# Weight tiles of a fused attention and feed-forward kernel: casting DMAs from GpSimd's queue in place of sync-queue loads and GpSimd casts

## Chip, cores and metric

One core of a Trainium2 chip. The metric is the device time of one execution in microseconds. Profiles are one profiled execution each; their times count from the start of the span.

## The reference, cut

Attention over 8 batches x 8 heads (512 local tokens in a window of 32, 32 global tokens, head size 64), then a feed-forward layer on the 4352 x 512 result:

```python
s_ll = np.where(np.abs(pos[:, None] - pos[None, :]) <= 32, s_ll, -1e9)
a_l = softmax(concat([s_lg, s_ll]));  out_l = a_l @ concat([v_g, v_l])
...
h = x @ w_in                       # w_in 512 x 2048
g = h * np.clip(h + 3, 0, 6) / 6
return g @ w_out                   # w_out 2048 x 512
```

All inputs are fp32. The kernel computes in half precision, so both weight matrices (4 MB each) have to become fp16 in SBUF.

## The kernel before: the parts that matter

Heads are handled in pairs, four pairs to a batch (`NM = 4`). Each weight matrix is cut into 16 tiles of 128 x 512. A tile of w_in is numbered `i = 4*qd + m`: `m` is the block of the contraction, `qd` the quarter of the 2048 columns. One feed-forward unit `u1(c)` multiplies column block `c` of w_in and so needs the four tiles of quarter `c // 4`: blocks 0 to 3 need tiles 0 to 3, block 4 is the first to need tiles 4 to 7.

```python
def stage():                       # 16 staging buffers of 128 x 512 fp32
    return wrk.tile([P, 512], FP32, tag="stg", name="stg", bufs=NSTG)

def load_w(kind, i):               # sync queue, plain DMA into staging
    t = stage()
    nc.sync.dma_start(out=t, in_=moe_w_in[...])      # or moe_w_out[...]
    w_st[kind, i] = t

def cast_w(kind, i, eng):          # GpSimd: staging fp32 -> home fp16
    eng.tensor_copy(out=o, in_=w_st[kind, i])
...
# sync queue, in program order (cut): k, q, v of pairs 0 to 3, then
for i in range(4): load_w("in", i)
load_g(1, 4, "kg"); load(4, "kq")
for i in range(4, 8): load_w("in", i)
load(5, "kq"); load(4, "v")
for i in range(8, 12): load_w("in", i)
...
# GpSimd, in program order (cut); first() is the v cast and a shifted copy
cast(3, "kq", nc.gpsimd)
for p in range(1, NM): first(p, "v")
for i in range(4): cast_w("in", i, nc.gpsimd)
cast(4, "kq", nc.gpsimd); load_vg(1)
for i in range(4, 8): cast_w("in", i, nc.gpsimd)
...
# PE, in program order (cut)
emit_G(1, 4, "kg"); u1(3); kglob(1, nc.vector)
emit_T(4)                          # transposes of pair 4
u1(4)                              # first use of w_in tiles 4 to 7
emit_S4(4)                         # mask matmuls, then the scores of pair 4
emit_T(5); ...
```

The orders of all engines are pinned, so an engine runs its instructions in just this order.

The softmax here doesn't subtract the row's maximum and nothing guards it: scores larger than these inputs give would overflow.

## Time and profile before

| | before |
|---|---|
| median of the fast runs | 317.62 us (317.42 to 318.07; the first run, 523.46, is no fast run; with it the median is 317.85) |
| span in the profile | 315.8 us, mean granted clock 0.998 |
| PE / VectorE / ScalarE / GpSimd busy | 96% / 68% / 63% / 48% |
| PE's work in the first 50 us, counted in columns | about 35 us (the five tens of the prediction add up to 32.5: its count leaves the 64-row matmuls out) |

To read it: PE is the bound after about 50 us; before that PE, ScalarE and VectorE wait for each other. The weights come by this list of DMA issues (columns: what, queue, kind and count, KB of one, median us from issue to landing):

```profile
stg<-in_moe_w_in_dram SPq DMA_DIRECT2D x16, 256.0 KB, 6.0
stg<-in_moe_w_out_dram SPq DMA_DIRECT2D x16, 256.0 KB, 5.1
```

### The profile page before, as it was taken

Reading aid. Unit: us, or ns where it says so; the run is one execution under the profiler, and the core shown is the slowest. Engines: PE = TensorE matmul, PEld = TensorE weight load, DVE = VectorE, ACT = ScalarE, POOL = GpSimd, SP = SyncE. Lnnn points to the kernel's source line nnn. Section 1 sums busy time; section 2 is a strip of 40 time slices with the busy share of each in tenths; the row PEclk is TensorE's granted clock in tenths of the full one; section 3 lists DMA queues with packets and bytes.
Section 4 is the critical chain, followed back from the end, with each engine's and each line's share of the span. In section 5 each row is a group of like instructions: output and inputs, shape, how many; then the busy total and the mean of one; then the engine's idle time right before and its main releaser. Section 6 shows DMA issues by size and latency. Waiting matters only on the chain.

```text
span 315.8 us, 7343 instructions
## 1 busy us (share of the span) xinstructions
PE 304.3 (96%) x2688; PEld 161.9 (51%) x2688; DVE 213.9 (68%) x484; ACT 200.1 (63%) x417; POOL 152.6 (48%) x273
## 2 busy tenths in 40 slices
PE   6898899999999999999999999999999999999995
PEld 4554555545555555555555555555555544448444
DVE  5678688898765799569945996468943962479101
ACT  6657877887444985479844993589556941579000
POOL 3878987599866475764574558542511000000000
PEclk9999999999999999999999999999999999999999
DMA  7999999999999999999997999896642002100131
GB/s 207 243 295 333 302 300 317 213 185 211 217 201 238 180 183 191 180 229 193 181 154 152 215 187 205 177 232 106 114 103 86 17 19 83 66 2 1 37 98 66
DMA packets 140260, 53.05 MB, mean 168 GB/s; under 512 B 127552, under 2 KB 131904, under 8 KB 140224
## 3 DMA queue, kind: packets, MB, share of 16 engines
q1 hardware_dynamic: 138048, 52.32, 78.3%
q0 software_dynamic: 2176, 0.26, 2.0%
q8 instruction: 21, 0.34, 0.5%
q14 instruction: 15, 0.12, 0.2%
HBM read 35.13 MB, written 8.91 MB: 139 GB/s over the span
## 4 chain that ended last, share of the span: by engine, by line
PE 81%; DVE 8%; ACT 6%; issue 2%; DMA 2%; SPq 0%; POOL 0%
PE po L488 34%; PE psH L472 32%; PE psS L297 3%; DVE gt L479 3%; PE pav L383 2%; PE pav L386 2%; ACT t L477 2%; DVE xn L391 2%; DMA stg<-in_q_l_dram 2%; DVE E L304 2%; PE psSG L357 1%; PE psS L326 1%; ACT E L335 1%; PE po L500 1%; ACT E L301 1%
## 5 line engine op out<-in xcount | busy, mean ns | idle before, releaser
L488 PE MATMUL po<-wout,gt 128*128 128x512 f16 x528 | 122.6, 379 | 0.0
L472 PE MATMUL psH<-xt,win 128*128 128x512 f16 x512 | 119.6, 379 | 1.4 <-POOL win L174 1.0
L479 DVE SCALAR_TENSOR_TENSOR gt<-t,psH 128x512 f16<-128x512 f32 (+1 forms) x144 | 90.1, 652 | 20.9 <-ACT t L477 19.8
L477 ACT ACTIVATE t<-psH,half_col 128x512 f32<-128x512 f32 (+1 forms) x144 | 91.8, 670 | 18.0 <-PE psH L472 16.8
L472 PEld LDWEIGHTS <-win 128*128 128x128 f16 x576 | 53.1, 98 | 52.8 <-POOL win L174 1.8
L488 PEld LDWEIGHTS <-gt 128*128 128x128 f16 x528 | 48.4, 98 | 52.2
L304 DVE TENSOR_TENSOR E<-E,mk 128x512 f16<-128x512 f16 x96 | 51.3, 569 | 30.4 <-ACT E L301 29.0
L301 ACT ACTIVATE E<-psS 128x512 f16<-128x512 f32 x96 | 49.9, 605 | 13.5 <-PE psS L297 13.4
L492 ACT COPY ot<-po 128x512 f32<-128x512 f32 x16 | 9.4, 586 | 58.6 <-PE po L488 53.1
L140 POOL CAST kn<-stg 128x512 f16<-128x512 f32 x31 | 19.8, 640 | 34.7 <-DMA stg<-in_k_l_dram 33.1
L391 DVE TENSOR_TENSOR xn<-pav,rc 128x256 f16<-128x256 f32 x64 | 26.1, 422 | 1.3
L409 POOL TENSOR_TENSOR s<-Eg 128x128 f32<-128x128 f16 x24 | 10.4, 434 | 33.8 <-ACT Eg L358 32.6
L492 DVE COPY ot<-po 128x512 f32<-128x512 f32 x17 | 11.7, 690 | 21.2 <-PE po L488 21.1
L140 POOL CAST qn<-stg 128x512 f16<-128x512 f32 x31 | 20.3, 656 | 11.3 <-DMA stg<-in_q_l_dram 11.3
L140 POOL CAST vt<-stg 128x512 f16<-128x512 f32 x32 | 21.1, 658 | 9.7 <-DMA stg<-in_v_l_dram 9.4
L144 POOL COPY vb<-vt 64x512 f16<-64x512 f16 x32 | 20.2, 631 | 2.1
L383 PE MATMUL pav<-vt,E 128*128 128x65 f16 x256 | 20.1, 194 | 0.0
L386 PE MATMUL pav<-vb,E 128*128 128x65 f16 x256 | 19.9, 195 | 0.0
L335 ACT ACTIVATE E<-psS 128x512 f16<-128x512 f32 x32 | 16.9, 600 | 4.8 <-PE psS L326 4.8
L383 PEld LDWEIGHTS <-E 128*128 128x128 f16 x256 | 17.9, 99 | 3.4
L386 PEld LDWEIGHTS <-E 128*128 128x128 f16 x256 | 16.8, 97 | 3.2
L297 PEld LDWEIGHTS <-kT 64*128 64x128 f16 x384 | 10.9, 94 | 10.1 <-issue 8.1
(93 smaller groups left out, 274.1 us busy)
## 6 DMA issues: line engine op xcount, KB each, us to landing
stg<-in_k_l_dram SPq DMA_DIRECT2D x32, 256.0 KB, 3.5
stg<-in_q_l_dram SPq DMA_DIRECT2D x32, 256.0 KB, 4.1
stg<-in_v_l_dram SPq DMA_DIRECT2D x32, 256.0 KB, 4.9
out_dram<-ot SPq DMA_DIRECT2D x23, 256.0 KB, 3.6
stg<-in_moe_w_in_dram SPq DMA_DIRECT2D x16, 256.0 KB, 6.0
stg<-in_moe_w_out_dram SPq DMA_DIRECT2D x16, 256.0 KB, 5.1
out_dram<-ot SPq DMA_DIRECT2D x8, 192.0 KB, 3.9
out_dram<-ot SPq DMA_DIRECT2D x16, 64.0 KB, 2.4
```

The lines of the kernel that those rows point to most:

```text
L140: eng.tensor_copy(out=o, in_=s[c + "f"])
L297: nc.tensor.matmul(out=pss[2 * ch + e][:, w * P:(w + 1) * P], lhsT=kT[r, c0:c0 + P], rhs=qT[r, w * P:(w + 1) * P])
L301: nc.scalar.activation(out=E[:, ch, e], in_=pss[2 * ch + e], func=EXP, scale=qk_scale)
L304: nc.vector.tensor_tensor(out=E[:, ch, e], in0=E[:, ch, e], in1=mk[:, ch].rearrange("p w c -> p (w c)"), op=mult)
L383: nc.tensor.matmul(out=o, lhsT=E[:, 0, e, w * P:(w + 1) * P], rhs=vt[:, w, m, c], start=True, stop=False, skip_group_check=True)
L386: nc.tensor.matmul(out=o, lhsT=E[:, 1, e, w * P:(w + 1) * P], rhs=vb[:, (w - 1) % NT, m, c], start=False, stop=True, skip_group_check=True)
L391: nc.vector.tensor_tensor(out=xn[:, 2 * w2:2 * w2 + 2].rearrange("p w (e d) -> p w e d", e=2), in0=po[:, :, 1:1 + P].rearrange("p w (e d) ...
L472: nc.tensor.matmul(out=ps[:, 0:n], lhsT=w_in_t[m][:, c * P:(c + 1) * P], rhs=rhs(m), start=(m == 0), stop=(m == NM - 1), skip_group_check= ...
L477: nc.scalar.activation(out=t1[:, 0:n], in_=ps[:, 0:n], func=RELU, bias=half_col, scale=1.0 / 6.0)
L479: nc.vector.scalar_tensor_tensor(out=gts[c][:, 0:n], in0=t1[:, 0:n], scalar=1.0, in1=ps[:, 0:n], op0=amin, op1=mult)
L488: nc.tensor.matmul(out=po[t][:, 0:dm], lhsT=gts[c][:, t * P:(t + 1) * P], rhs=w_out_t[c // 4][:, c % 4], start=(c == 0), stop=(c == NC - 1))
L492: (nc.scalar.copy if t % 2 else nc.vector.tensor_copy)(out=ot, in_=po[t][:, 0:dm])
```

## The change

The intent: a DMA issued from GpSimd can cast, so the 32 staging loads and the 32 casts become 32 loads straight into the fp16 homes; the sync queue is left to k, q and v. The core of the diff (removals in the sync queue's list, and most of GpSimd's list, are cut):

```diff
-    def load_w(kind, i):
-        t = stage()
...
-    def cast_w(kind, i, eng):
...
+    def load_w(kind, *ts):
+        for i in ts:
+            if kind == "in":
+                qd, m = divmod(i, NM)
+                cs = slice(qd * 512, (qd + 1) * 512)
+                nc.gpsimd.dma_start(out=w_in_t[m][:, cs], in_=moe_w_in[m * P:(m + 1) * P, cs])
+            else:
+                nc.gpsimd.dma_start(out=w_out_t[i // 4][:, i % 4], in_=moe_w_out[i * P:(i + 1) * P, :])
...
     cast(3, "kq", nc.gpsimd)
-    for p in range(1, NM):
-        first(p, "v")
-    for i in range(4):
-        cast_w("in", i, nc.gpsimd)
+    load_w("in", 0, 1)
+    first(1, "v")
+    load_w("in", 2)
+    first(2, "v")
+    load_w("in", 3)
+    first(3, "v")
+    load_w("in", 4, 5)
     cast(4, "kq", nc.gpsimd)
     load_vg(1)
-    for i in range(4, 8):
-        cast_w("in", i, nc.gpsimd)
+    load_w("in", 6, 7)
     cast(5, "kq", nc.gpsimd)
+    load_w("in", 8, 9)
...
```

The orders of PE, VectorE and ScalarE stay as they were.

More of the change, by code (lines that the diff above doesn't have):

```diff
@@ L155, in load_vg @@
         nc.gpsimd.dma_start(out=vg[rg, b], in_=v_g[b].rearrange("h s d -> s h d"))
-    w_st = {}
-    def load_w(kind, i):
-        t = stage()
-        if kind == "in":
-            qd, m = divmod(i, NM)
-            nc.sync.dma_start(out=t, in_=moe_w_in[m * P:(m + 1) * P, qd * 512:(qd + 1) * 512])
-        else:
-            nc.sync.dma_start(out=t, in_=moe_w_out[i * P:(i + 1) * P, :])
-        w_st[kind, i] = t
-    def cast_w(kind, i, eng):
-        if kind == "in":
-            qd, m = divmod(i, NM)
-            o = w_in_t[m][:, qd * 512:(qd + 1) * 512]
-        else:
-            o = w_out_t[i // 4][:, i % 4]
-        (eng.copy if eng is nc.scalar else eng.tensor_copy)(out=o, in_=w_st[kind, i])
+    def load_w(kind, *ts):
[6 more added lines that the diff above has]
+                nc.gpsimd.dma_start(out=w_out_t[i // 4][:, i % 4], in_=moe_w_out[i * P:(i + 1) * P, :])
     gst = {}
@@ L539 @@
         load(p, "v")
-    for i in range(4):
-        load_w("in", i)
     load_g(1, 4, "kg")
     load(4, "kq")
-    for i in range(4, 8):
-        load_w("in", i)
     load(5, "kq")
     load(4, "v")
-    for i in range(8, 12):
-        load_w("in", i)
     load(6, "kq")
@@ L552 @@
     load(7, "kq")
-    for i in range(12, NC):
-        load_w("in", i)
     load(6, "v")
@@ L557 @@
     load_g(0, 4, "qg")
-    for i in range(8):
-        load_w("out", i)
     load(2 * NM, "kq")
-    for i in range(8, NC):
-        load_w("out", i)
     load(2 * NM, "v")
@@ L621 @@
     cast(3, "kq", nc.gpsimd)
-    for p in range(1, NM):
-        first(p, "v")
-    for i in range(4):
-        cast_w("in", i, nc.gpsimd)
+    load_w("in", 0, 1)
[5 more added lines that the diff above has]
+    load_w("in", 4, 5)
     cast(4, "kq", nc.gpsimd)
     load_vg(1)
-    for i in range(4, 8):
-        cast_w("in", i, nc.gpsimd)
+    load_w("in", 6, 7)
     cast(5, "kq", nc.gpsimd)
+    load_w("in", 8, 9)
     first(4, "v")
     ones_v(1, nc.gpsimd)
-    for i in range(8, 12):
-        cast_w("in", i, nc.gpsimd)
+    load_w("in", 10, 11)
     cast(6, "kq", nc.gpsimd)
+    load_w("in", 12, 13)
     first(5, "v")
+    load_w("in", 14, 15)
     cast(7, "kq", nc.gpsimd)
-    for i in range(12, NC):
-        cast_w("in", i, nc.gpsimd)
+    load_w("out", 0, 1)
     first(6, "v")
+    load_w("out", 2, 3)
     first(7, "v")
+    load_w("out", 4, 5)
     vgsum(0, nc.gpsimd)
@@ L644 @@
     vgsum(1, nc.gpsimd)
+    load_w("out", 6, 7)
     load_vg(2)
-    for i in range(8):
-        cast_w("out", i, nc.gpsimd)
+    load_w("out", 8, 9, 10, 11)
     cast(2 * NM, "kq", nc.gpsimd)
-    for i in range(8, NC):
-        cast_w("out", i, nc.gpsimd)
+    load_w("out", 12, 13, 14, 15)
     units += moe_units(lambda mm: xts[0][mm], Sl, local_dests(0), early=True)
```

## The prediction

> **What bounds the kernel now.** I began with the page of the profile: busy shares first, then the 40 slices, to see whether one limit holds over the whole span.
>
> ```profile
> PE 304.3 (96%) x2688; PEld 161.9 (51%) x2688; DVE 213.9 (68%) x484; ACT 200.1 (63%) x417; POOL 152.6 (48%) x273
> ...
> PE   6898899999999999999999999999999999999995
> ...
> POOL 3878987599866475764574558542511000000000
> ...
> DMA  7999999999999999999997999896642002100131
> ```
>
> PE is busy 96%, yet those ends are modelled, so I also counted work: columns streamed over 2.4 columns per ns (the rate that eight 512-column matmuls in 1.73 us show), half for 64-row ones that run in pairs. This gives 3.8 of the first 10 us, 5.3 of the second, then 7.5, 7.3, 8.6 and 10.2. So PE has about 17 us of slack before 50 us and almost none after. Whatever this change does must happen before about 50 us: from there the matmuls stand back to back, and a shift at 50 us reaches the end unchanged. The DMA engines are full from about 4 us to 100 us.
>
> Next, the source view of the cast that the change removes (L174, GpSimd), and who waited for it:
>
> ```profile
> L174 POOL CAST win<-stg x16: 609/614/807, 17.8 to 38.9; 128x512 f16<-128x512 f32 x16
> L174 POOL CAST wout<-stg x16: 611/616/619, 45.0 to 57.6; 128x512 f16<-128x512 f32 x16
> ...
>   PEld L472: 1.8, 2
>   PE psH L472: 1.0, 2
> ```
>
> The 32 casts cost GpSimd 0.61 us each, 19.7 us in all. PE waited for them 1.0 us in total. The timeline of PE shows where: the third and fourth matmul of column block 4, which need the w_in tiles 6 and 7.
>
> ```profile
> 26.08 0.39 PE L472 MATMUL psH<-xt,win 128*128 128x512 f16 x1 [0.45 <-POOL win L174]
> 27.03 0.39 PE L472 MATMUL psH<-xt,win 128*128 128x512 f16 x1 [0.56 <-POOL win L174]
> 27.26 1.03 PE L310 MATMUL psS<-mneg,ident 128*128 128x512 f16 x4
> 28.48 0.62 PE L326 MATMUL psS<-qT,kT 64*128 64x128 f16 x16 [0.20 <-DVE kT L252]
> ```
>
> Last, the chain of work that ended last, in order of time, over the same stretch. It passes through VectorE and not through the cast: the scores at 28.48 wait for kT, behind the three gt and four kgT copies. Even the 1.0 us of PE is therefore not wholly on the path.
>
> ```profile
> 24.05 1.88 DVE gt L479 x3
> ...
> 26.93 0.69 DVE gt L479
> ...
> 27.83 0.61 DVE kT L252
> 28.44 0.05 issue
> 28.48 0.44 PE psS L326 x8
> ```
>
> **What the Trainium skill says.** (1) "DMA: Bandwidth & Descriptors", section "SWDGE vs HWDGE vs iDMA": a cast inside a DMA can only be issued from GpSimd, whose cores write the descriptors. That is why these loads leave the sync queue. The kernel already has eight such loads, vg from v_g (fp32 to half precision), so the trace holds a sample. (2) Same page, "Issuing engines are not separate DMA queues": all queues run on the same 16 DMA engines and interleave, so a second queue adds no bandwidth. The trace agrees: where the engines are full, a vg load lands in 5.9 to 7.9 us, where they are less so in 3.0 to 3.3 us. (3) "Perfetto Trace Analysis", section "DMA Instruction — SWDGE (GPSIMD)": the recorded time of such an instruction is descriptor writing, not data movement. So what GpSimd pays is the 577 to 739 ns of the tile view below. (4) "SBUF — State Buffer", section "A bandwidth-pool intuition that's wrong (but worth ruling out)": descriptor writing can be held up while VectorE has the shared port. No sign of it here: the issue at 23.21 took 0.59 us right beside a VectorE cast of 0.70 us that began at 22.78.
>
> ```profile
> L155 POOL DMA_DIRECT2D vg<-in_v_g_dram x8: 577/600/739, 1.5 to 184.9; - x8
> ...
> DMA to landing us min/median/max: 3.0/3.9/7.9
> ```
>
> **The change part by part.**
>
> *GpSimd: removed and added.* Out go 32 casts x 0.615 = 19.7 us; in come 32 issues. A vg issue makes 272 packets in 0.60 us; a weight tile has 128 rows, so I take 0.6 us as an upper estimate: 19.2 us. GpSimd's work hardly changes. What it loses are waits: 1.9 us before win casts and 1.1 us before wout casts, data not yet there. None of it sets the end by itself.
>
> *Sync queue: removed.* 32 issues of 256 KB leave. Of 30 transfers issued between 12.3 and about 36 us in that queue, 16 were w_in. In the new order k, q and v of pairs 4 to 7 follow directly on v of pair 3. The sync timeline shows 0.7 us from one issue to the next where it is limited by bandwidth, so pair 4 comes about 4 x 0.7 = 3 us earlier and later pairs more. PE waited only 0.16 us for a q cast of pairs 4 to 7, so I credit 0.2 us.
>
> *HBM bytes.* The same fp32 bytes are read; only the written half shrinks. I credit nothing.
>
> *Weight tiles: moved.* This is the term that counts. The order of PE, VectorE and ScalarE is unchanged; GpSimd's is new. I walk down GpSimd's new order with the old durations. The third q cast ends at 13.5 us (as before). Issue w0, w1: to 14.7. v cast and shift of pair 1 (1.3): 16.0. Issue w2: 16.6. Pair 2: 17.9. Issue w3: 18.5. Pair 3: 19.8. Issue w4, w5: 21.0. k, q casts of pair 4: 22.2. The vg load and w6, w7: 24.0. To the start of each issue I add a landing of 5 to 7 us in this full stretch, an estimate from the 5.9 to 7.9 us of vg there: a weight tile has 9 packets per engine against vg's 17, but 2 KB each. So:
> - w0, w1 land at 19 to 21; needed at 20.7: in time, or half a microsecond late;
> - w2 issued at 16.0, lands 21 to 23, needed 22.2; w3 issued at 17.9, lands 23 to 25, needed 23.7: up to 1.3 us late;
> - w6 and w7 issued at 22.8 and 23.4, land 28 to 30.5; in the old run w7 was used at 27.03.
>
> The scores at 28.48 could have borne block 4 ending some 0.2 us later. With w7 at 29.3 (middle), block 4 ends 0.2 us after that and four mask matmuls (0.9 us) follow: 30.4, against 28.48, so 1.9 us late. The later v casts of pairs 1 to 3 fit: shift of pair 3 at 19.8 against 17.75, used at 20.23. From w8 on there is room: w8 to w11 are issued by 29, land by 36, and are used from 38.6; w12 to w15 by 34 and 41, used after 45; w_out by about 50 and used from 50.6 on, where only its first four tiles are needed at once and those are issued by 39.
>
> Some of the 1.9 us comes back while PE stands, because VectorE and ScalarE work off their queue; ScalarE's four exponentials then follow at the old pace, so I give back 0.3 us, and 0.2 us for the earlier q. Sum: 1.9 - 0.5 = +1.4 us at least. To the middle I add 1.0 us for the chance, below, that casting transfers are slower than plain ones. 318.1 + 2.4 = 320.5 us.
>
> **The rivals.**
>
> *A: nothing is seen, or a slight gain.* The GpSimd queue has its own ring, and the engines alternate between rings, so the weights need not stand behind eight earlier sync loads. If they land in 4 us, w7 is there at 27.4, where the old one was: 317 to 318 us. For it: 3.0 to 3.3 us in less loaded stretches. Against: 5.9 and 6.6 us for the two vg loads of just this time. A gain over 2% would need 6.4 us out of a start-up whose chain alternates over PE, ScalarE and VectorE and hardly touches the removed casts; I see no source for it.
>
> *B: a cast costs the DMA engines extra.* The queue table for the first 20 us gives the casting queue 2.5% of 16 engines for 272 packets: 0.025 x 320 / 272 = 29 ns for 256 bytes read; the plain queue has 85.1% x 320 / 7942 = 34 ns for 570 bytes on average. So a cast of 256 bytes isn't slow, but the bound is loose: at 256 bytes per 29 ns, a 2 KB row would take 235 ns and a tile of eight rows per engine 1.9 us, 32 tiles 60 us, and w7 would come near 34 us instead of 29. At half of a plain rate (about 0.7 us per tile becoming 1.4 us) w7 lands at 32 to 33: +5 us, 323. At the loose bound the w_out tiles come late too: 328 to 335. The vg rows are too short to tell.
>
> *C: GpSimd becomes the wait.* [...]If landings stretch, GpSimd stops at an issue and holds up the casts behind it. With landings of 6 us and at most 8 issues in 10 us this doesn't bind; with B it would, and would add to it.
>
> **Range and chances.** A gives 317 to 318, the main path 319 to 321, B 323 and over. I give A about 0.25, the main path 0.45, B and C 0.3, of which two thirds end beyond 324.4 (2% slower). Predicted 320.5 us, 316.8 to 326.5 for 8 in 10; faster 0.03, within 2% 0.77, slower 0.20.
>
> **What would show each step right or wrong.** In the changed profile: 32 weight issues on GpSimd of about 0.6 us and no L174 cast; their landing 5 to 7 us before 30 us (4 or less: A; 8 or more: B); the idle time of L472 now laid to the DMA of win, largest at the w7 matmul; the scores of pair 4 at about 30.4 instead of 28.48; and the same distance from there to the end (318 - 28.5), within 1 us. Packets of the casting queue well over 100 ns each would speak for B. The prediction is wrong if PE waits for w_out after 50 us, if GpSimd stands long at issues, or if the start-up gets shorter.

## The result, and the profile after

The changed kernel is correct and takes 321.2 us median (319.94 to 321.79, 4 runs), against 317.62. The ratio is 1.0105, 95% interval 1.0062 to 1.0148. A ratio here is the mean time of one kernel's runs over the mean of the other's of the same rounds, so not quite the ratio of the medians. Executions over 1.5% slower than the fastest of the same kernel are left out of the means. That is a loss of about 3.3 us.

The issues in the page of the changed kernel: the weights now stand under GpSimd's queue (the size is now the written one).

```profile
win<-in_moe_w_in_dram POOLq DMA_DIRECT2D x16, 128.0 KB, 6.3
wout<-in_moe_w_out_dram POOLq DMA_DIRECT2D x16, 128.0 KB, 5.4
```

The source view of the w_in issues, now line 162, gives the cost of one to GpSimd, 537 ns, and who waited; nothing on GpSimd stood idle for them, and nobody waited for the w_out issues at all.

```profile
L162 POOL DMA_DIRECT2D win<-in_moe_w_in_dram x16: 530/537/735, 12.6 to 33.1; - x16
...
who waited for it (us, times):
  PEld L462: 4.0, 5
  PE psH L462: 2.3, 4
```

PE's timeline of the changed kernel, the same stretch as before. In brackets stands the idle time before an instruction and what ended it. The four matmuls of block 4 now each wait for a landing; the scores of pair 4 (the last line) start at 30.46 instead of 28.48 us.

```profile
26.09 0.39 PE L462 MATMUL psH<-xt,win 128*128 128x512 f16 x1 [0.31 <-DMA win<-in_moe_w_in_dram]
26.87 0.39 PE L462 MATMUL psH<-xt,win 128*128 128x512 f16 x1 [0.40 <-DMA win<-in_moe_w_in_dram]
28.45 0.39 PE L462 MATMUL psH<-xt,win 128*128 128x512 f16 x1 [1.19 <-DMA win<-in_moe_w_in_dram]
29.28 0.39 PE L462 MATMUL psH<-xt,win 128*128 128x512 f16 x1 [0.43 <-DMA win<-in_moe_w_in_dram]
...
30.46 0.62 PE L316 MATMUL psS<-qT,kT 64*128 64x128 f16 x16
```

The chain that ended last runs through that tile. In the kernel before it ran through VectorE here; now it is GpSimd's issues (the one at 21.61 us is that of tile 6, just ahead of tile 7's at 22.14), a landing of 7.1 us, and PE:

```profile
21.61 0.54 POOL win L162
22.14 7.09 DMA win<-in_moe_w_in_dram
...
29.28 0.39 PE psH L462
29.67 0.86 PE psS L300 x4
```

I followed the start of each later group of scores in both timelines. The distance to the kernel before is 1.98 us at pair 4, 1.97 at 70 us, 1.67 from 81 us on and 2.37 from 126 us to the end (the spans: 318.2 - 315.8 = 2.4). So of the profiled 2.4 us, 2.0 are made before 31 us. Two things are not explained by them: that profiled run is the fastest of the four (319.94), and the step from 1.67 to 2.37. The step lies beside a group of VectorE multiplications with two SBUF inputs. The first fence is VectorE's timeline before, the second after:

```profile
111.97 1.95 DVE L304 TENSOR_TENSOR E<-E,mk 128x512 f16<-128x512 f16 x4
```

```profile
113.63 2.67 DVE L294 TENSOR_TENSOR E<-E,mk 128x512 f16<-128x512 f16 x4
```

It takes 0.72 us longer after; GpSimd is at work through most of both stretches. Other kernels below show the same step at 0.3 to 0.5 us, and the step of -0.3 us at 81 us too. Which GpSimd instructions fall on these multiplications may matter, but no experiment isolated that: the cause of the step stays open.

### The profile page after: what moved, and what is told of

It reads as the page before. It is cut to its first block, busy times and chain, and to the rows that moved or that the text cites. A ratio compares the mean times of both kernels' runs of the same rounds, so it can differ in the third digit from the quotient of the medians.

```text
span 318.2 us, 7275 instructions
## 1 busy us (share of the span) xinstructions
PE 305.5 (96%) x2688; PEld 162.4 (51%) x2688; DVE 215.1 (68%) x484; ACT 199.9 (63%) x417; POOL 149.6 (47%) x273
## 4 chain that ended last, share of the span: by engine, by line
PE 78%; DVE 8%; ACT 5%; DMA 3%; issue 3%; POOL 1%; SPq 0%; ACTq 0%
PE po L478 35%; PE psH L462 29%; PE psS L287 3%; DVE gt L469 3%; DMA win<-in_moe_w_in_dram 2%; PE pav L376 2%; PE pav L373 2%; ACT t L467 2%; DVE xn L381 2%; ACT E L325 1%; PE psSG L347 1%; DMA stg<-in_q_l_dram 1%; PE psS L316 1%; PE po L490 1%; ACT E L291 1%
## 5 line engine op out<-in xcount | busy, mean ns | idle before, releaser
L469 DVE SCALAR_TENSOR_TENSOR gt<-t,psH 128x512 f16<-128x512 f32 (+1 forms) x144 | 90.1, 652 | 22.2 <-ACT t L467 20.9
L140 POOL CAST kn<-stg 128x512 f16<-128x512 f32 x31 | 19.1, 615 | 35.0 <-DMA stg<-in_k_l_dram 27.7
```

The lines of the kernel that those rows point to most:

```text
L140: eng.tensor_copy(out=o, in_=s[c + "f"])
L469: nc.vector.scalar_tensor_tensor(out=gts[c][:, 0:n], in0=t1[:, 0:n], scalar=1.0, in1=ps[:, 0:n], op0=amin, op1=mult)
```

## The experiments

Ratios are against the kernel before in the same rounds. "Tile 7" is the start of the PE matmul that uses it, "scores" the start of the scores of pair 4, both from PE's timeline; the clock is the mean granted clock of the profiled run.

| kernel | tile 7 | scores | clock | median us | ratio, 95% interval |
|---|---|---|---|---|---|
| before | 27.03 | 28.48 | 0.998 | 317.62 | |
| changed | 29.28 | 30.46 | 0.999 | 321.2 | 1.0105, 1.0062 to 1.0148 |
| changed, again | 29.15 | 31.40 | 0.994 | 321.63 | 1.0111, 1.0085 to 1.0137 |
| only w_out changed | 26.73 | 28.31 | 0.999 | 317.9 | 0.9988, 0.9961 to 1.0014 |
| only w_in changed | 29.32 | 31.57 | 0.995 | 321.48 | 1.0108, 1.0072 to 1.0144 |
| tiles issued earlier | 27.80 | 28.99 | 1.000 | 318.4 | 1.0028, 0.9992 to 1.0065 |
| PE kept busy | 29.61 | 30.79 | 1.000 | 319.94 | 1.0076, 1.0049 to 1.0103 |
| 12 staging buffers | 29.85 | 32.10 | 0.994 | 322.12 | 1.0136, 1.0110 to 1.0161 |
| 12 buffers, w_in tiles 0 to 7 uncast | 29.87 | 31.58 | 0.995 | 320.89 | 1.0107, 1.0073 to 1.0141 |
| tiles 0 and 1 earlier too | 28.42 | 29.61 | 1.000 | 319.53 | 1.0056, 1.0028 to 1.0084 |
| 12 buffers, sync loads held back | 28.42 | 30.33 | 0.995 | 320.17 | 1.0058, 1.0023 to 1.0092 |
| held back and earlier | in time | 28.66 | 0.999 | 318.81 | 1.0029, 0.9994 to 1.0064 |

### The changed kernel once more

> The changed kernel once more, for its scatter. Theory: ratio to the kernel before 1.007 to 1.012; the scores of pair 4 (16 matmuls of 64x128) start at 30.0 to 31.0 us in the profile against 28.5 us before, because the w_in tile 7 lands at about 29.2 us; runs differ by the landing of that tile. Rival (the loss is made after 50 us, by a lower granted clock or by the DMA engines): those scores start at 28.5 to 29 us in some run and the time is still 320 us or more.

Measured: the ratio as expected. The scores missed the range, 31.40 us, although tile 7 came no later than in the first profile. PE's timeline of this run shows where the difference is made:

```profile
28.24 0.46 PE L462 MATMUL psH<-xt,win 128*128 128x512 f16 x1 [1.09 <-DMA win<-in_moe_w_in_dram]
29.15 0.61 PE L462 MATMUL psH<-xt,win 128*128 128x512 f16 x1 [0.45 <-DMA win<-in_moe_w_in_dram]
29.55 1.91 PE L300 MATMUL psS<-mneg,ident 128*128 128x512 f16 x4
31.40 0.82 PE L316 MATMUL psS<-qT,kT 64*128 64x128 f16 x16
```

The matmul on tile 7 lasts 0.61 instead of 0.39 us, and the four mask matmuls 1.91 us. The windows view of the same run gives the reason (the columns: stretch; its length, then busy time and count of PE, weight loads, VectorE, ScalarE and GpSimd; granted clock; DMA share; GB/s):

```profile
26.00:28.00 2.00, 0.48 (x2) 0.10 (x1) 1.93 (x6) 0.95 (x3) 1.96 (x5) 1.00 1.24 231
...
29.00:30.00 1.00, 0.85 (x3) 0.30 (x4) 0.14 (x1) 0.20 (x1) 0.00 (x0) 0.50 1.21 259
30.00:31.00 1.00, 1.00 (x4) 0.28 (x2) 0.48 (x1) 0.49 (x1) 0.00 (x0) 0.50 1.21 211
31.00:32.00 1.00, 1.00 (x17) 0.60 (x16) 0.21 (x1) 0.00 (x0) 0.00 (x0) 0.57 1.20 229
```

After a stretch with 0.48 of 2 us busy, the granted clock falls to 0.50 and stays there from about 28.4 to about 31.9 us. How sparse PE's work has to be for that, these runs don't decide. In a kernel shown further down (tiles 0 and 1 earlier too), PE was busy only 0.39 of the same 2 us, and the clock did not fall:

```profile
26.00:28.00 2.00, 0.39 (x1) 0.10 (x1) 1.94 (x6) 0.00 (x0) 0.61 (x1) 1.00 1.28 255
...
29.00:30.00 1.00, 1.00 (x18) 0.49 (x17) 0.43 (x1) 0.54 (x1) 0.96 (x3) 1.00 1.20 244
```

The distance to the kernel before is then 3.10 us, against 1.97 in the first profile: between these two profiles the fall costs 1.1 us. A fall of 0.5 for 3.4 us of 318 lowers the mean clock by 0.005, so it can be seen in runs without a trace. Of the ten runs of the changed kernel in both tests, nine have a mean clock of 0.992 to 0.995 and one 0.999: the profiled one of 319.94 us. The eleven runs of the kernel before in this test have 0.998 to 1.000; in the two later tests, three of its 22 runs have 0.994 or 0.995 and took 319.10 to 319.58 us, so it falls there too, but seldom.

### One half of the change alone

Only w_out: w_in is loaded and cast as before.

```diff
 # against the kernel before
-    for i in range(8):             # sync queue, and range(8, NC) likewise
-        load_w("out", i)
-    for i in range(8):             # GpSimd, and range(8, NC) likewise
-        cast_w("out", i, nc.gpsimd)
+    load_w("out", 0, 1)            # casting DMAs, at the places of the changed kernel
```

> Only the w_out half of the change: w_in by the sync queue and GpSimd casts as before, w_out by casting DMAs. Theory (all of the loss comes from w_in tiles before 30 us): ratio to before 0.998 to 1.003. Rival (the loss is from casting DMAs in general, or from their use of the DMA engines after 35 us): 1.005 or more.

Measured: 0.9988, scores at 28.31 us. In the profile PE waits for one w_out tile:

```profile
60.88 0.38 PE L497 MATMUL po<-wout,gt 128*128 128x512 f16 x1 [0.52 <-DMA wout<-in_moe_w_out_dram]
```

The distance to the kernel before goes from -0.17 us at pair 4 to +0.49 at 70 us. The last w_out load is issued at 53.4 us here and at 49.7 in the changed kernel, where nobody waits for one. The time does not show this wait.

Only w_in: the reverse edit, in which w_out keeps its staging loads and casts.

> Only the w_in half of the change: w_in by casting DMAs, w_out by the sync queue and GpSimd casts as before. Theory: the whole loss, ratio to before 1.007 to 1.012, scores of pair 4 at about 30.4 us. Rival (w_out matters): 1.005 or less.

Measured: 1.0108, the whole loss; tile 7 at 29.32. The scores, at 31.57, are later than expected, again with a fall of the clock (mean 0.995). So the loss is made by w_in; the 16 casting DMAs for w_out show none in the time (interval up to 1.0014).

### Tiles issued earlier in GpSimd's order

```diff
     first(1, "v")
-    load_w("in", 2)
+    load_w("in", 2, 3)
     first(2, "v")
-    load_w("in", 3)
+    load_w("in", 4, 5)
     first(3, "v")
-    load_w("in", 4, 5)
+    load_w("in", 6, 7)
     cast(4, "kq", nc.gpsimd)
     load_vg(1)
-    load_w("in", 6, 7)
```

> The changed kernel with weight tiles issued earlier in GpSimd's order: tile 3 with 2, tiles 4 and 5 before the v cast of pair 3, tiles 6 and 7 before the k and q casts of pair 4, so tile 7 is issued about 1.3 us sooner (at about 20.4 instead of 22.1 us). Theory (the place in GpSimd's order sets the landing): tile 7 lands 1 to 1.5 us sooner, the scores of pair 4 start at 29.0 to 29.6 us, and the time is 1 to 1.5 us below the changed kernel (ratio to before 1.003 to 1.006). Rival (the DMA engines or the casting transfer set the rate at which tiles land, not the issue): tile 7 lands at 29 us all the same, and the time stays at 1.009 to 1.011.

Measured: tile 7 at 27.80, scores at 28.99, ratio 1.0028. Moving five issues forward (tiles 6 and 7 past two casts and the vg load) gives back about three quarters of the loss. That is a little more than expected: scores and ratio lie just below their ranges, and in five runs the fall of the clock is gone as well. These five of its six runs have a clock of 0.998 or more; four of them lie between 317.63 and 318.5 us, but one took 321.33 us, so there is a scatter that isn't the clock's too.

A step further, tiles 0 and 1 were issued before the v cast of pair 0 as well:

```diff
+    load_w("in", 0, 1)
     first(0, "v")
     cast(3, "kq", nc.gpsimd)
-    load_w("in", 0, 1)
```

> As the kernel with tiles issued earlier, and w_in tiles 0 and 1 issued before the v cast of pair 0 as well, where GpSimd waits for data; tile 7 is then issued at about 19.5 us instead of 20.5. Theory: tile 7 lands at about 27 us, PE no longer waits for it beyond what VectorE makes it wait, the scores of pair 4 start at 28.3 to 28.8 us and the ratio to before is 0.998 to 1.002. Rival (the bandwidth of the DMA engines in this stretch is the limit): the scores start at 29 us or later, 1.003 or more, because the v casts of pairs 1 to 3 or the tiles are late instead.

Measured: scores at 29.61, ratio 1.0056; the expectation of the theory failed. GpSimd's timeline of this kernel shows why no time was won: the two issues delay the v and k casts behind them, so that tiles 6 and 7 were issued at 19.83 us, in the kernel above at 19.92 us.

```profile
10.00 1.14 POOL L162 DMA_DIRECT2D win<-in_moe_w_in_dram  x2
11.13 0.69 POOL L140 CAST vt<-stg 128x512 f16<-128x512 f32 x1
...
19.83 1.05 POOL L162 DMA_DIRECT2D win<-in_moe_w_in_dram  x2
```

From the same issue time tile 7 was used 0.6 us later. The issue is not all: how fast the DMA engines come to a tile counts too.

### PE kept busy while it waits

```diff
     emit_T(4)
-    u1(4)
+    for m in range(NM):
+        warm_up(5)                 # five 128x256 matmuls on zeros
+        u1(4, range(m, m + 1))
```

> The changed kernel with PE kept busy while it waits for w_in tiles 4 to 7: five small matmuls on zeros (128x256, some 0.5 us in all) ahead of each of the four matmuls of column block 4; no load moves. Theory (in most runs of the changed kernel the idle time of PE before 30 us makes the granted clock fall to 0.5 for about 3.5 us, which costs about 1 us on top of the late tile): no run with a mean clock below 0.998, the scores of pair 4 at 30.3 to 30.8 us as in the one profile of the changed kernel without the fall, and the time 0.5 to 1.2 us below the changed kernel (ratio to before 1.006 to 1.009). Rival (the clock does not matter, or the extra matmuls cost what they save): 1.010 or more.

Measured: ratio 1.0076, and a mean clock of 1.000 in all six runs. The scores start at 30.79 us and the later distance is 2.3 us. That is 0.3 us more than in the first profile because tile 7 came 0.3 us later (issued at 22.4, landing in 7.2 us); PE waited 0.29 us for it after the last five extra matmuls, so these did not delay it. Its windows, to be held against those of the run above:

```profile
26.00:28.00 2.00, 1.81 (x15) 1.16 (x12) 1.93 (x6) 0.84 (x3) 1.54 (x7) 1.00 1.24 205
...
29.00:30.00 1.00, 0.71 (x5) 0.24 (x4) 0.04 (x1) 0.00 (x0) 1.00 (x2) 1.00 1.15 270
30.00:31.00 1.00, 1.00 (x12) 0.41 (x12) 0.24 (x1) 0.69 (x1) 1.00 (x3) 1.00 1.16 315
```

With the tile just as late, about 1 us of the loss goes when PE doesn't idle. The intervals of the two ratios overlap a little, but the clock stayed up in all six runs. That is the second term of the loss.

### Is the cast slow, or do the tiles queue?

The control has fewer staging buffers; the other kernel, on top of it, loads w_in tiles 0 to 7 without the cast. Its matmuls read the upper halves of the fp32 values as bf16, every second element.

```diff
-    NSTG = 16
+    NSTG = 12
```

> The changed kernel with 12 staging buffers instead of 16, so the sync queue cannot run as far ahead with the later k, q and v while the first weight tiles are loaded; it is also the control of the next kernel. Theory that the weight tiles land late because they share the DMA engines with sync loads pulled ahead: landing of the w_in tiles shorter (median under 6 us against 6.3 to 6.6), tile 7 lands up to 1 us sooner, and the ratio to before 1.004 to 1.009. Rival (landing of casting loads is a fixed latency): landing and time unchanged, 1.010 to 1.012.

```diff
+    w_in_f = [const(f"winf{m}", [P, dff // 2], FP32) for m in range(NM)]
...
+    nc.gpsimd.dma_start(out=(w_in_f if qd < 2 else w_in_t)[m][:, ds], in_=moe_w_in[...])
...
+    return w_in_f[m].bitcast(mybir.dt.bfloat16)[:, 2 * c * P + 1:2 * (c + 1) * P:2]
```

> As the kernel with 12 staging buffers, but w_in tiles 0 to 7 are loaded without the cast, from the same queue at the same places: fp32 rows of 2 KB into fp32 homes, of which the matmuls read the upper halves as bf16 (the result is rounded more coarsely, and may differ from the reference a little). Theory (the place in the order counts, not the cast): tile 7 lands within 0.7 us of the kernel with 12 buffers, and the time is within 1 us of it. Rival (the cast slows the DMA engines): the tiles land at least 1 us sooner, and the time falls by 1 us or more.

Measured: with 12 buffers 1.0136, outside both expectations. In it the sync queue had come to pair 6's k by 17.03 us, against 16.35 us in the changed kernel, so this edit didn't hold back what it was to hold back and decides nothing about sharing; the start of its first weight issue, 13.32 against 12.57 us, is more than enough for tile 7 being 0.6 us later. As a control it serves. The matmul on tile 7 in the control, then in the kernel without the cast:

```profile
29.85 0.61 PE L462 MATMUL psH<-xt,win 128*128 128x512 f16 x1 [0.34 <-DMA win<-in_moe_w_in_dram]
```

```profile
29.87 0.39 PE L469 MATMUL psH<-xt,winf 128*128 128x512 f16 x1 [0.34 <-DMA winf<-in_moe_w_in_dram]
```

Cast or not, the tile comes at the same time, although the uncast one was issued 0.8 us sooner (22.2 against 23.0 us): it took 7.6 us to land, the cast one 6.8. The median of the eight is 7.2 us uncast, 6.7 cast. The edit changes one more thing: an uncast tile writes 256 KB instead of 128. The time was 0.9 us lower by the ratios, with overlapping intervals and in a mix of runs with and without the fall of the clock. So a load with the cast is no slower, as a whole, than one without it from the same queue, and that is not what makes the tiles late. The result was correct within tolerance.

### The sync queue held back

k, q and v of pairs 4 to 7 get four staging buffers of their own, so that the sync queue has to stop after k and q of pairs 4 and 5:

```diff
-    NSTG = 16
+    NSTG = 12
...
-    t = stage()
+    t = (wrk.tile([P, 512], FP32, tag="stgb", name="stg", bufs=4) if NM <= p < 2 * NM
+         else stage())
```

> As the kernel with 12 staging buffers, but k, q and v of pairs 4 to 7 go through four buffers of their own, so the sync queue stops after k and q of pairs 4 and 5 (at about 15.5 us) until GpSimd casts them at 20 us, instead of pulling five more tiles ahead while w_in tiles 2 to 7 are loaded. Theory that the weight tiles land late because they share the DMA engines with the loads that the emptied sync queue pulls ahead: tiles 4 to 7 land 4.5 to 6 us after their issue instead of 6.5 to 7.5, tile 7 at 27 to 28.3 us, the scores of pair 4 at 28.5 to 29.5 us, ratio to before 1.000 to 1.006. Rival (a casting load has a fixed latency of some 6 us while the engines are busy with anything): tile 7 lands at 29 us or later, ratio 1.009 or more.

Measured: the landing of the eight tiles issued from 12 to 23 us falls to 5.4 us median, from 6.7 in the control and 6.9 and 7.3 in the two profiles of the changed kernel. Tile 7 is used at 28.42, 0.1 us over the expected range; the ratio is 1.0058, within it. The scores, 30.33, missed theirs mostly by the fall of the clock (five of six runs at 0.994 or 0.995). The sync timeline shows the pause:

```profile
14.63 0.47 SPq L125 DMA_DIRECT2D stg<-in_q_l_dram  x1
20.27 0.37 SPq L128 DMA_DIRECT2D stg<-in_v_l_dram  x1
```

Tiles 4 and 5 were issued within the pause and landed in 4.2 and 5.1 us (6.2 and 7.3 in the control). Tiles 6 and 7, issued after the sync queue had gone on, took 6.4 and 6.5 us, over the expected 4.5 to 6. So part of the landing is sharing: the sync queue, freed of the weights, runs ahead with loads that nobody needs yet, over the same engines. But tile 7 comes 1.4 us sooner than in the control mostly because it was issued 1.1 us sooner. Both remedies together:

> Both remedies: the earlier issue of tiles 3 to 7 and the four buffers of their own for pairs 4 to 7. Theory: tile 7 lands at about 26 to 27 us, PE waits no longer than in the kernel before, the scores of pair 4 start at 28.2 to 28.7 us and the time equals before (ratio 0.997 to 1.002); it can't be much faster, because that start is then set by VectorE's copies. Rival (the held-back loads of pairs 4 to 7 come too late instead): 1.004 or more.

Measured: PE no longer waits for tiles 4 to 7; it waits 1.15 us for VectorE's kT, as the chain of the kernel before has it. PE's timeline:

```profile
25.22 1.25 PE L463 MATMUL psH<-xt,win 128*128 128x512 f16 x4
26.30 1.21 PE L301 MATMUL psS<-mneg,ident 128*128 128x512 f16 x4
28.66 0.62 PE L317 MATMUL psS<-qT,kT 64*128 64x128 f16 x16 [1.15 <-DVE kT L243]
```

Tile 7 was issued at 20.4 us here and in the kernel with tiles issued earlier; with the sync queue held back (and 12 buffers) it landed in 5.6 us, without in 7.3. This pair shows the sharing for tile 7 itself. The scores are 0.18 us behind the kernel before, and the ratio is 1.0029, interval 0.9994 to 1.0064: neither theory is ruled out by the time alone. No version here beats the kernel before; with the tiles in time, VectorE's copies set the start of the scores.

## Why the prediction was right

The predicted time was 320.5 us in a range of 316.8 to 326.5; measured were 321.2. Its main step, the late w_in tiles, held. That the number came so near is partly luck: terms offset each other. As a rise it was 2.4 us on a base of 318.1 (the median known then), and some 3.3 us on 317.7 (the mean) were measured.

- **PE, VectorE and ScalarE keep their order; what counts lies before 50 us.** Right: 2.0 of the 2.4 us of the profile are made before 31 us, and with w_out alone the time does not change (0.9988). The count of columns behind it is off: with the 64-row matmuls at half, as it says, the first 50 us hold about 35 us of work and some 15 of slack, not 17. The step does not depend on it.
- **w_in tiles 6 and 7 come late, block 4 stalls, scores at about 30.4.** Right, and tested: 30.46 in the profile, and issuing the tiles earlier takes most of the loss away. Two of its terms were off in opposite directions: tile 7 was issued by 22.1 us and not 23.4 (12.57 instead of 13.5 at the start, and 0.54 instead of 0.6 us per issue), and landed 7.1 us later instead of about 6. So its 29.3 us for tile 7 was met (29.28) by luck. One sign was missed: the longest wait was for tile 6 (1.19 us), not tile 7 (0.43).
- **0.5 us come back through VectorE, ScalarE and earlier q.** Wrong: the distance was 1.98 at pair 4 and 1.97 at 70 us.
- **1.0 us for slow casts (rival B).** Wrong: without the cast tile 7 comes at the same time, from an earlier issue even.
- **Missing: the granted clock.** While PE idles for the late tiles, the clock falls to 0.50 for some 3.4 us in nearly all runs and costs 1.1 us or more. By luck this filled the place of the 1.0 us for slow casts. The check "same distance to the end" could not have shown it, since the fall comes before the scores.
- **Rival A (landing in 4 us).** Wrong: 6.9 to 7.3 us median for these tiles. The sync queue pulled ahead shares the engines; held back, they land in 5.4 us. The 3.0 to 3.3 us that spoke for A were misread: the row of the page shows the DMA engines full to about 165 us, not 100, and the vg loads at 71, 124 and 153 us landed in 3.2 to 3.3 us at a DMA share of 0.96 to 1.26. What was lower there is what the engines moved, 185 to 220 GB/s against 302 and 327 where vg took 7.9 and 6.6 us.
- **Rival C (GpSimd stands at issues).** Not seen: no idle time before either kind of issue.

Put together for a usual run: 2.0 us late tile and 1.1 us clock make the 3.1 us by which the second profile lags (318.9 - 315.8). The means of the runs ask for 3.3 to 3.6 us. The 1.1 us of one pair of profiles may be low: the nine runs of the changed kernel with a fall average 321.5 us, 1.6 above the one without, and in the six other kernels that have both sorts of runs, those at about 0.995 are 1.0 to 1.9 us slower on average. Those runs sorted themselves, so this is no experiment. That 5.4 us of landing remain even with the sync queue held back is not taken apart further; the plain w_in loads of the sync queue in the kernel before took 6.0 us median, and no run put such loads at the places of GpSimd's.

## What to carry to other kernels

Taking instructions off GpSimd, which didn't set the end, won nothing here; what the change really moved was the time at which the first tiles land. So walk through the new order of the issuing engine and set each landing against its first use. The emptied queue didn't leave the DMA engines empty: it ran ahead, and the loads that had become urgent landed later for it (7.3 against 5.6 us for tile 7). And price a stall of PE with the clock after it: here 3.4 us at half rate followed most stalls and cost a microsecond or more.

## What the Trainium skill lacked or had wrong

- "TensorE: Matmul & The Clock Gate", section "Why this matters for your kernels", asks for no idle gaps of PE over about 3 us. Here the clock fell to 0.50 although the longest gap before the fall was 1.09 us, so this row alone would not have warned. A rule by PE's busy share doesn't come out of these runs either: of 3.4 us in this stretch, PE was busy 1.63 us in the run with the fall (24.9 to 28.3) and 1.55 us in the one without (25.0 to 28.4). The page's half rate and its window of about 3.4 us, section "What's actually happening", agree with what was seen: 0.50 for 3.4 us in each of the five profiles with a fall.
- "DMA: Bandwidth & Descriptors" has no cost for a cast in a DMA, and no landing time for a GpSimd load beside a busy sync queue. Here 2 KB rows cast to 1 KB land no later than uncast ones from the same queue (6.8 against 7.6 us from issue for tile 7), and a load that reads 256 KB landed in 6.9 to 7.3 us median, in 5.4 us with the sync queue held back.
